# A linear-attention block with SwiGLU, forward and backward, on one core: warm-up and z inside the k/q loop, reloads moved to other queues, a ring filled ahead, a padded last K tile

## The chip, the cores and the metric

The kernel runs on one core of one Trainium2 chip. The metric is the device time of a whole execution in microseconds (us); lower is better. TensorE (PE) multiplies matrices and reads its left operand by separate weight loads (PEld), VectorE (DVE), ScalarE (ACT) and GpSimd (POOL) do elementwise work, and SyncE (SP), ACT and POOL issue DMAs from queues that run in order.

## The reference, cut to what matters

The input x has 2048 rows (S) of 640 features (D). There are 32 heads of 20 features, and F = 1728 hidden features.

```python
def A(x, wqkv, wo):                    # linear attention
    q, k, v = split_heads(x @ wqkv)
    pq, pk = phi(q), phi(k)            # phi(t) = where(t > 0, t + 1, exp(t)) + 1e-6
    kv = einsum("bhsd,bhse->bhde", pk, v)
    z = einsum("bhsd->bhd", pk)
    o = (pq @ kv) / (pq . z + 1e-6)    # per head and row
    return merge_heads(o) @ wo
def B(x, w_gate, w_up, w_down):
    return (silu(x @ w_gate) * (x @ w_up)) @ w_down
h = x + A(layernorm(x), wqkv, wo)
out = h + B(layernorm(h), w_gate, w_up, w_down)
```

The kernel returns `out` (out_0) and the gradients of x, wqkv, wo, w_gate, w_up and w_down for a given `grad_out`, all in bf16.

## The kernel before, in words

Rows are cut into 16 tiles of 128 (ST), features into 5 tiles (DT). A product with 640 output columns runs as two halves of 320 columns (`mm_row`, L115), each accumulated over its K tiles in one bank of a PSUM buffer; all matmuls share four such buffers. In SBUF, `strips` has four large buffers (tag S) and `big` five (tag B). The stages follow each other on TensorE:

- **k/q loop** (L256 to L268, 8.6 to 61.7 us). For each tile LayerNorm 1 (`ln_stats`, `ln_rstd`: VectorE's `lnv` L130, then POOL's power L131), the normalised `xn` (L226), five transposes `ps_t` (L230) copied by ScalarE, then k and q (`ps_kq`, 20 matmuls) and phi: two ScalarE operations per half of k/q from PSUM, two on VectorE. The order of PE, DVE and ACT is written out by hand. x's first tile is loaded first.
- **z and masks** (L270 to L278, 61.7 to 67.3 us). `ps_z` sums pk over all rows by 32 matmuls with a matrix of ones; five matmuls with E (the 0/1 matrix of heads, made on POOL, L185 to L190) make the head masks.
- **middle** (to 175 us). `ps_y`, `ps_kvt`, `ps_w2`, `ps_a` with LayerNorm 2, and between them `ps_dm`, the gradient of the product of gate and up; for groups 1 to 3 it is stored in `scr_dm`.
- **four F groups** (L403 to L487, 175 to 477 us) of 448, 448, 448 and 384 columns. A loop over pairs of tiles computes gate and up (`pg`, `pu`), four ScalarE operations and seven VectorE operations (L440 to L446) that make m, dg and du; dg and du (`dd`) are transposed on SP into `stg` (L449) and stored by POOL in `scr_dT` (L450). Then SP transposes the weights into `wgT` (L458), and `dw` (L460 to L473) multiplies, evicts `dwev` and stores it from POOL. A group after the first needs `dm_s`, loaded on SP at L410 in the group's first lines. `ps_dw` begins with m_s, so with 28 matmuls that don't need the loop's last pair.
- **dhn** (L534 to L579, 481 to 621 us). `cols`, the transposed dg and du of two tiles, is loaded on POOL (`load_cols`, L519); each tile is 54 matmuls with wgT, and lagging behind it `ps_dp`.
- **the small matrices** (to 656 us): `ps_gt`, `ps_dkvt`, `ps_wv2` (whose WV2 is transposed into WK2 on SP), then `ps_dz`, VectorE's `dzE` (L625) and `ps_dzb`.
- **dwqk, dk, dxn** (L630 to L698, to 798 us). `dwqk(0)` stores the gradient of wq; a loop over tiles makes dk (from `xnT_r`, loaded on ACT's queue, and `pkr`, loaded on POOL) and, three tiles later, `ps_dxn` from three transposed pieces in `ring` (dk four slots, pk and dq three each), all transposed by SP.
- **down** (L725 to L745, to 873 us): `ps_o` with 14 K tiles per half, the last of 64 rows (L734), `dwo` and `dwv` between the tiles.

Within the hand-ordered stretches the named engines keep the order of the code: PE, DVE and ACT in the k/q loop, PE and DVE in the middle, SP in the F groups and later. Otherwise a scheduler orders the instructions. DMAs of the hardware queues take turns over eight completion semaphores (lanes) in the order of the program, so a new one also waits for the earlier one on its lane.

Of the kernel before, what the change touches and what calls it, by code (L numbers as in the profile page):

```python
# [20 lines left out]
def kernel(  # L21
# [106 lines left out]
    def ln_rstd(mv, mean, rstd, t0, nt):  # L128
        v = small.tile([P, 4], FP32, name="lnv", tag="lnv")
        nc.vector.tensor_scalar(out=v[:, :nt], in0=mv[:, :nt, 1], scalar1=1e-5, scalar2=None, op0=ALU.add)  # L130
        nc.gpsimd.tensor_tensor(out=rstd[:, t0:t0 + nt], in0=v[:, :nt], in1=nhalf[:, :nt], op=ALU.pow)  # L131

    def ln_bwd(ps, xhat, rstd_col, resid, dst, pool):
# [10 lines left out]
        nc.vector.tensor_tensor(out=dst, in0=a[:], in1=resid, op=ALU.add)  # L144

# [28 lines left out]
    for t0 in range(4, ST, 2):  # L174
# [4 lines left out]
    ident = const.tile([P, P], BF16, name="ident")  # L179
    make_identity(nc, ident[:])  # L180
    nhalf = const.tile([P, 4], FP32, name="nhalf")
    nc.vector.memset(nhalf[:], -0.5)
    ones = const.tile([P, P], BF16, name="ones")
    nc.vector.memset(ones[:], 1.0)
    E = const.tile([H, D], BF16, name="E")  # L185
    nc.gpsimd.memset(E[:], 1.0)
    nc.gpsimd.affine_select(out=E[:], in_=E[:], pattern=[[1, D]], compare_op=ALU.is_ge,
                            fill=0.0, base=0, channel_multiplier=-Dh)
    nc.gpsimd.affine_select(out=E[:], in_=E[:], pattern=[[-1, D]], compare_op=ALU.is_ge,
                            fill=0.0, base=Dh - 1, channel_multiplier=Dh)  # L190
# [29 lines left out]
    def ln1_stats(t):  # L220
        mvs[t] = small.tile([P, 4, 2], FP32, name="mv", tag="mv")
        ln_stats(x_tm[t // 8][:, t % 8, :], mvs[t][:, 0, :])
        ln_rstd(mvs[t], None, rstd1, t, 1)
# [32 lines left out]
    with tc.manual_schedule(engines={EngineType.PE, EngineType.DVE, EngineType.Activation}):  # L256
        ln1_stats(0)
# [12 lines left out]
    ps = mm("ps_z")  # L270
    mm_row(ps, lambda t: ones[:], lambda t, n0, n1: pk[:, t, n0:n1], ST)
    nc.scalar.copy(out=half(zb[:]), in_=row(ps))

    for i in range(DT):
        e0, e1 = head_range(i)
        ps = mm("ps_mask")
        nc.tensor.matmul(ps[:, 0, :e1 - e0], lhsT=E[:, i * P:(i + 1) * P], rhs=E[:, e0:e1], start=True, stop=True)
        nc.scalar.copy(out=mask[:, i, :e1 - e0], in_=ps[:, 0, :e1 - e0])  # L278
# [55 lines left out]
    with tc.manual_schedule(engines={EngineType.PE, EngineType.DVE}):  # L334
# [35 lines left out]
        for t in range(ST + 2):  # L370
            if t < ST:
# [8 lines left out]
                ln_rstd(mv, None, rstd2, t, 1)  # L380
# [16 lines left out]
    with tc.manual_schedule(engines={EngineType.SP}):  # L397
# [5 lines left out]
        wgu = {0: load_wgu(0), 1: load_wgu(1)}  # L403
        for g in range(4):
            w = GW[g]
            if g == 0:
                dm_s = dm0
            else:
                dm_s = strips.tile([P, ST, GM], BF16, name="dm_s", tag="S")
                nc.sync.dma_start(out=dm_s[:, :, :w], in_=scr_dm_v[:, :, GO[g]:GO[g] + w])  # L410
# [5 lines left out]
            for t in range(0, ST, 2):  # L416
# [25 lines left out]
                nc.vector.tensor_tensor(out=du, in0=m, in1=dmv, op=ALU.mult)  # L442
                nc.vector.tensor_tensor(out=m, in0=m, in1=u, op=ALU.mult)  # L443
# [64 lines left out]
    with tc.manual_schedule(engines={EngineType.SP}):  # L508
# [6 lines left out]
        colp = {}  # L515
        pqr = {}
        dh1Ts = {}

        def load_cols(p):  # L519
            colp[p] = strips.tile([P, 2, NKT, P], BF16, name="cols", tag="S")  # L520
            nc.gpsimd.dma_start(out=colp[p][:], in_=scr_dT[2 * p:2 * p + 2].rearrange("t p k c -> p t k c"))
# [9 lines left out]
        load_cols(0)  # L531
# [80 lines left out]
        nc.gpsimd.dma_start(out=mat_v(scr_dKVT), in_=dKVT[:])  # L612
        wvk = strips.tile([P, 2, DT, D], BF16, name="wvk", tag="S")
# [8 lines left out]
        dzE = wk("dzE")  # L622
        ps = mm("ps_dz")
        mm_row(ps[:H], lambda t: nS1[:, t, :], lambda t, n0, n1: pqs_tm[:, t, n0:n1], ST)
        nc.vector.tensor_tensor(out=half(dzE[:H, :]), in0=row(ps)[:H], in1=half(E[:]), op=ALU.mult)  # L625
# [12 lines left out]

        G = mat("G")
        tr_mat(G, scr_GT)  # L640
# [4 lines left out]
        dwqk(0, 0, 4)  # L645

        dk = big.tile([P, ST, D], BF16, name="dk", tag="B")
        ring = strips.tile([P, 10, DT, P], BF16, name="ring", tag="S")
# [127 lines left out]
```

## Time and profile before

| | |
|---|---|
| median of 3 runs | 878.8 us (878.8 to 879.22) |
| the profiled execution, its own time | 884.85 us |
| its span in the profile | 883.0 us |
| mean granted TensorE clock | 0.980 |
| TensorE busy | 842.5 us, 95% |
| VectorE, ScalarE, POOL busy | 422.8, 299.8, 183.3 us |
| DMA traffic | 175.66 MB, 199 GB/s |

Times in the profile run from the start of the span. A row of a timeline gives start, length, engine, line, operation, output <- inputs and, in brackets, how long the engine sat idle ahead of it and what released it. A row of the waits gives the total, the number of times and the longest. A row of the chain gives start, length and what ran.

### The profile page before, as it was taken

How to read it: one execution, taken by the hardware profiler on the slowest of the kernel's cores; microseconds unless marked ns; L12 is line 12 of the kernel's file. 1: busy time of each engine (PE TensorE's matmuls, PEld its weight loads, DVE VectorE, ACT ScalarE, POOL GpSimd, SP SyncE). 2: the span in 40 equal slices, each digit the busy share in tenths (PEclk: the TensorE clock that was granted, in tenths of full speed). 3: DMA queues.
4: the chain of work that ended last, by engine and by line, in shares of the span. 5: the costliest groups of instructions: out<-in, count | busy, mean ns of one | idle time of the engine just before them, and what ended most of it. 6: DMA issues, size and time to landing. Idle time of an engine off the chain costs nothing.

```text
span 883.0 us, 13963 instructions
## 1 busy us (share of the span) xinstructions
PE 842.5 (95%) x5461; PEld 528.9 (60%) x5461; DVE 422.8 (48%) x864; ACT 299.8 (34%) x421; POOL 183.3 (21%) x321
## 2 busy tenths in 40 slices
PE   6999999999998899999998999999999699999995
PEld 4666655655554455555654777777766477776663
DVE  6969645886019405902910254786811366421111
ACT  5982433293157016513701222232221133331010
POOL 2110111213242331231225021111002111113140
PEclk9999999999999899999998999999999799999998
DMA  9999969999998893994799777773599699786971
GB/s 300 205 301 271 217 166 245 208 220 219 225 272 201 210 269 80 215 226 117 188 235 257 226 171 227 162 177 94 93 249 237 138 176 178 152 201 138 228 209 49
DMA packets 304066, 175.66 MB, mean 199 GB/s; under 512 B 250464, under 2 KB 289680, under 8 KB 304000
## 3 DMA queue, kind: packets, MB, share of 16 engines
q1 hardware_dynamic: 273856, 91.51, 52.8%
q0 software_dynamic: 19296, 72.60, 26.0%
q10 hardware_dynamic: 10848, 10.65, 4.3%
q8 instruction: 43, 0.70, 0.3%
q14 instruction: 23, 0.19, 0.1%
HBM read 53.72 MB, written 64.01 MB: 133 GB/s over the span
## 4 chain that ended last, share of the span: by engine, by line
PE 69%; DMA 14%; DVE 10%; issue 4%; ACT 1%; POOL 1%; SPq 0%; DVEq 0%; POOLq 0%; ACTq 0%
PE ps_dhn L119 14%; PE ps_dw L469 10%; PE ps_dxn L689 8%; PE ps_dm L293 7%; DMA stg<-dd 6%; PE ps_o L735 6%; PE ps_dwqk L119 4%; DMA scr_dT<-stg 3%; PE ps_gt L528 2%; PE ps_y L119 2%; PE ps_dp L119 2%; PE ps_a L119 2%; PE pg L420 2%; PE ps_dk L119 2%; PE pu L425 2%
## 5 line engine op out<-in xcount | busy, mean ns | idle before, releaser
L119 PE MATMUL ps_dhn<-wgT,cols 128*128 128x320 bf16 x864 | 122.0, 303 | 3.8 <-DMA cols<-scr_dT 3.8
L469 PE MATMUL ps_dw<-dd,hn 128*128 128x448 bf16 (+1 forms) x640 | 118.8, 346 | 0.0
L119 PEld LDWEIGHTS <-cols 128*128 128x128 bf16 x864 | 85.5, 99 | 38.4 <-DMA cols<-scr_dT 4.2
L469 PEld LDWEIGHTS <-hn 128*128 128x128 bf16 x640 | 62.6, 98 | 54.2
L471 ACT CAST dwev<-ps_dw 128x896 bf16<-128x896 f32 (+1 forms) x20 | 17.6, 878 | 164.7 <-PE ps_dw L469 155.1
L471 DVE CAST dwev<-ps_dw 128x896 bf16<-128x896 f32 (+3 forms) x12 | 10.9, 906 | 127.1 <-PE ps_dw L469 107.1
L469 PE MATMUL ps_dw<-m_s,dh 128*128 128x448 bf16 (+1 forms) x320 | 63.9, 357 | 7.2 <-DVE m_s L443 7.2
L735 PE MATMUL ps_o<-wd,mT 128*128 128x320 bf16 x448 | 67.7, 300 | 0.0
L450 POOL DMA_DIRECT2D scr_dT<-stg x64 | 34.6, 541 | 158.9 <-DMA stg<-dd 151.6
L689 PEld LDWEIGHTS <-ring 128*128 128x128 bf16 x480 | 48.1, 100 | 28.9 <-DMA ring<-dq 9.0
L420 PE MATMUL pg<-wgu,hnT 128*128 128x448 bf16 (+1 forms) x320 | 63.6, 346 | 0.0
L425 PE MATMUL pu<-wgu,hnT 128*128 128x448 bf16 (+1 forms) x320 | 63.6, 346 | 0.0
L293 PE MATMUL ps_dm<-wdT,dh2T 128*128 128x448 bf16 (+1 forms) x320 | 62.0, 346 | 0.0
L689 PE MATMUL ps_dxn<-wqkvT,ring 128*128 128x320 bf16 x320 | 53.3, 307 | 8.7 <-DMA ring<-dq 8.7
L735 PEld LDWEIGHTS <-mT 128*128 128x128 bf16 x448 | 41.3, 97 | 26.3 <-issue 8.4
L469 PEld LDWEIGHTS <-dh 128*128 128x128 bf16 x320 | 32.0, 100 | 37.1 <-issue 11.8
L425 PEld LDWEIGHTS <-hnT 128*128 128x128 bf16 x320 | 31.3, 98 | 27.1
L119 PE MATMUL ps_kq<-wqk,xnT 128*128 128x320 bf16 x320 | 47.5, 306 | 0.0
L420 PEld LDWEIGHTS <-hnT 128*128 128x128 bf16 x320 | 31.3, 98 | 27.1
L293 PEld LDWEIGHTS <-dh2T 128*128 128x128 bf16 x320 | 31.3, 98 | 25.1
L737 DVE TENSOR_TENSOR h1r<-ps_o,h1r 128x640 bf16<-128x640 f32 x16 | 13.2, 825 | 67.4 <-PE ps_o L735 62.6
L136 ACT ACTIVATE lb_dy<-ps_dhn,rstd 128x640 bf16<-128x640 f32 x16 | 12.7, 793 | 81.4 <-PE ps_dhn L119 81.4
(144 smaller groups left out, 1264.9 us busy)
## 6 DMA issues: line engine op xcount, KB each, us to landing
cols<-scr_dT POOLq DMA_DIRECT2D x8, 1728.0 KB, 9.2
scr_dT<-stg POOLq DMA_DIRECT2D x48, 224.0 KB, 2.8
scr_m<-m_s POOLq DMA_DIRECT2D x12, 448.0 KB, 4.3
scr_dm<-dmst ACTq DMA_DIRECT2D x16, 224.0 KB, 3.2
dm_s<-scr_dm SPq DMA_DIRECT2D x2, 1792.0 KB, 11.2
out_dram<-dwev POOLq DMA_DIRECT2D x30, 112.0 KB, 4.7
scr_dT<-stg POOLq DMA_DIRECT2D x16, 192.0 KB, 3.3
scr_xn<-xn SPq DMA_DIRECT2D x4, 640.0 KB, 5.7
```

What stands on the lines that cost most here:

```text
L119: nc.tensor.matmul(ps[:, ci, :320], lhsT=lhs(k), rhs=rhs(k, n0, n1), start=(start and k == 0), stop=(stop and k == n - 1))
L136: nc.scalar.activation(out=half(dy[:]), in_=row(ps), func=ACT.Copy, scale=rstd_col, accum_out=sums[:, 0:1])
L293: nc.tensor.matmul(ps[:, c, :w], lhsT=dh2T[:, kt, (t + c) * P:(t + c + 1) * P], rhs=wdT[g // 2][:, kt, o:o + w], start=(kt == 0), stop=(kt ...
L420: nc.tensor.matmul(pg[:, c, :w], lhsT=hnT[:, kt, (t + c) * P:(t + c + 1) * P], rhs=wg[:, kt, 0:w], start=(kt == 0), stop=(kt == DT - 1))
L425: nc.tensor.matmul(pu[:, c, :w], lhsT=hnT[:, kt, (t + c) * P:(t + c + 1) * P], rhs=wg[:, kt, w:2 * w], start=(kt == 0), stop=(kt == DT - 1))
L450: nc.gpsimd.dma_start(out=scr_dT[t + c, :, KO[g]:KO[g] + GK[g], :], in_=stg[:, :GK[g], :])
L469: nc.tensor.matmul(ps[:, c, :w], lhsT=lhs(t), rhs=rhs(t), start=(t == 0), stop=(t == ST - 1))
L471: copy(out=ev[:, :len(parts), :w], in_=ps[:, :len(parts), :w])
L528: nc.tensor.matmul(ps[:, ci, :320], lhsT=dh1[:, t, i * P:(i + 1) * P], rhs=pqs_tm[:, t, n0:n1], start=(t == 0), stop=(t == ST - 1))
L689: nc.tensor.matmul(ps[:, ci, :320], lhsT=lhs[:, i, :], rhs=rhs[:, i, n0:n1], start=(k == 0 and i == 0), stop=(k == 2 and i == DT - 1))
L735: nc.tensor.matmul(ps[:, ci, :320], lhsT=mT[:kk, t % 4, j, :], rhs=wd[:kk, j, n0:n1], start=(j == 0), stop=(j == FT - 1))
L737: nc.vector.tensor_tensor(out=half(h1r[:]), in0=row(ps), in1=half(h1r[:]), op=ALU.add)
```

## The change

In the k/q loop, 48 matmuls of the identity with itself (`ps_warm`, never read) run on TensorE before the first transposes. The mask matmuls move ahead of the first k/q matmul, all five into one PSUM buffer. `ps_z` is opened before the loop and two of its matmuls follow tile t's k/q matmuls from t = 2 on, so one of the four PSUM buffers is held throughout. POOL's order is written out for ident and E, and `lnv` goes from VectorE to POOL (but for the first two tiles).

In the F groups the load of `dm_s` for the next group, and after the last group the first `cols`, are issued on ACT's queue right behind the group's loop; `cols` of tile pair 1 stays on POOL. VectorE's seven operations are reordered with an extra work tile `a`, so that none directly follows one it depends on. It takes a third buffer of the six that nsg, u and `dwev` share.

`ps_dz` and dzE go ahead of `ps_wv2`. The pk and dq pieces of the ring for tiles 0 to 2 are issued before the loop, and those of tile u + 3 once tile u's matmuls are issued. G's transposes move into the loop, behind those of KV and Y. `dwqk(0)` is cut 3, 1, 1 instead of 4, 1. The last K tile of `ps_o` has 128 rows, of which 64 in `wd` are set to zero. The last tile of the output is added and stored in two halves, from ACT's and SP's queues.

```diff
+        eng.tensor_scalar(out=v[:, :nt], in0=mv[:, :nt, 1], scalar1=1e-5, scalar2=None, op0=ALU.add)
...
+        ps = mm("ps_warm")
+        for _ in range(48):
+            nc.tensor.matmul(ps[:, 0, :P], lhsT=ident[:], rhs=ident[:], start=True, stop=True)
...
+        ps_z = mm("ps_z")
+        def z_mm(t):
+            for ci, (n0, n1) in enumerate(NCH):
+                nc.tensor.matmul(ps_z[:, ci, :320], lhsT=ones[:], rhs=pk[:, t, n0:n1],
+                                 start=(t == 0), stop=(t == ST - 1))
...
+            if t == 0:
+                masks()
             kq_mm(t)
             if t > 0:
                 kq_phi(t - 1)
+            if t > 1:
+                z_mm(t - 2)
         kq_phi(ST - 1)
...
-                nc.sync.dma_start(out=dm_s[:, :, :w], in_=scr_dm_v[:, :, GO[g]:GO[g] + w])
...
+                a = fw("a")[:, :, :w]
                 nc.vector.tensor_tensor(out=m, in0=m, in1=dg, op=ALU.mult)
+                nc.vector.tensor_tensor(out=a, in0=u, in1=dmv, op=ALU.mult)
                 nc.vector.tensor_tensor(out=nsg, in0=nsg, in1=m, op=ALU.mult)
                 nc.vector.tensor_tensor(out=du, in0=m, in1=dmv, op=ALU.mult)
+                nc.vector.tensor_tensor(out=nsg, in0=nsg, in1=dg, op=ALU.add)
                 nc.vector.tensor_tensor(out=m, in0=m, in1=u, op=ALU.mult)
-                nc.vector.tensor_tensor(out=nsg, in0=nsg, in1=dg, op=ALU.add)
-                nc.vector.tensor_tensor(out=dg, in0=u, in1=dmv, op=ALU.mult)
-                nc.vector.tensor_tensor(out=dg, in0=dg, in1=nsg, op=ALU.mult)
+                nc.vector.tensor_tensor(out=dg, in0=a, in1=nsg, op=ALU.mult)
...
+            if g < 3:
+                dm_s = strips.tile([P, ST, GM], BF16, name="dm_s", tag="S")
+                act_load(dm_s[:, :, :GW[g + 1]], scr_dm_v[:, :, GO[g + 1]:GO[g + 1] + GW[g + 1]])
+            else:
+                load_cols(0, act_load)
...
+        for v in range(3):
+            load_pqT(v)
         G = mat("G")
-        tr_mat(G, scr_GT)
...
-                    kk = P if j < 13 else 64
-                    nc.tensor.matmul(ps[:, ci, :320], lhsT=mT[:kk, t % 4, j, :], rhs=wd[:kk, j, n0:n1],
+                    nc.tensor.matmul(ps[:, ci, :320], lhsT=mT[:, t % 4, j, :], rhs=wd[:, j, n0:n1],
```

How the queues stand, in three places. The first is the turn from group 0 to group 1. Before, SP's queue (`w2t` and `hnT` belong to the middle; x16 stands for a run of like instructions):

```order
L389 DMA_TRANSPOSE hnT<-hn 128x5x128 x3
L393 DMA_TRANSPOSE w2t<-W_1333 128x5x128 x3
L156 DMA wgu<-in_B_w_up_dram 128x5x448
L449 DMA_TRANSPOSE stg<-dd 128x7x128 x16
L458 DMA_TRANSPOSE wgT<-wgu 128x7x128 x5
L410 DMA dm_s<-scr_dm 128x16x448
L155 DMA wgu<-in_B_w_gate_dram 128x5x448
```

Now ScalarE's queue, at the end of group 0's loop (L464 to L467 are its four operations per pair, L508 the evictions of dw):

```order
L464 ACTIVATE dd<-pg 128x2x448
L465 ACTIVATE nsg<-pg 128x896
L466 CAST m_s<-pg 128x896
L467 CAST u<-pu 128x896
L149 DMA dm_s<-scr_dm 128x16x448
L508 CAST dwev<-ps_dw 128x896 x5
```

The load has left SP, where it stood behind the 16 stg and 5 wgT transposes, and stands on ACT ahead of the five evictions. The second place is SP's queue after dhn, before:

```order
L502 DMA_TRANSPOSE wqkvT<-in_A_wqkv_dram 128x5x128 x15
L621 DMA_TRANSPOSE wvk<-wvk 128x5x128 x5
L502 DMA_TRANSPOSE G<-scr_GT 128x5x128 x5
L670 DMA_TRANSPOSE ring<-dk 128x5x128 x2
L673 DMA_TRANSPOSE ring<-scr_pk 128x5x128
L674 DMA_TRANSPOSE ring<-dq 128x5x128
```

And SP's queue there now (L670 and L671 are the new `load_pqT`, L704 the dk pieces):

```order
L539 DMA_TRANSPOSE wqkvT<-in_A_wqkv_dram 128x5x128 x15
L653 DMA_TRANSPOSE wvk<-wvk 128x5x128 x5
L670 DMA_TRANSPOSE ring<-scr_pk 128x5x128
L671 DMA_TRANSPOSE ring<-dq 128x5x128
L670 DMA_TRANSPOSE ring<-scr_pk 128x5x128
L671 DMA_TRANSPOSE ring<-dq 128x5x128
L670 DMA_TRANSPOSE ring<-scr_pk 128x5x128
L671 DMA_TRANSPOSE ring<-dq 128x5x128
L704 DMA_TRANSPOSE ring<-dk 128x5x128 x4
```

Six pieces that stood behind dk's now stand ahead of them, where G's five were. The third place is POOL's queue at the same point, before:

```order
L602 DMA scr_GT<-GT 128x5x640
L612 DMA scr_dKVT<-dKVT 128x5x640
L637 DMA out_dram<-dwqk 128x640 x3
L653 DMA pkr<-scr_pk 128x640 x2
L637 DMA out_dram<-dwqk 128x640
```

And POOL's queue there now (L665 is the dwqk store, L687 the load of pkr):

```order
L630 DMA scr_GT<-GT 128x5x640
L640 DMA scr_dKVT<-dKVT 128x5x640
L687 DMA pkr<-scr_pk 128x640
L665 DMA out_dram<-dwqk 128x640 x2
L687 DMA pkr<-scr_pk 128x640 x2
L665 DMA out_dram<-dwqk 128x640
```

The first load of pkr has moved from behind three dwqk stores to ahead of all of them.

More of the change, by code (lines that the diff above doesn't have):

```diff
@@ L256, with masks @@
     with tc.manual_schedule(engines={EngineType.PE, EngineType.DVE, EngineType.Activation}):
+        def masks():
+            ps = mm("ps_mask")
+            for i in range(DT):
+                e0, e1 = head_range(i)
+                pm = ps[:, i // 3, (i % 3) * 160:(i % 3) * 160 + e1 - e0]
+                nc.tensor.matmul(pm, lhsT=E[:, i * P:(i + 1) * P], rhs=E[:, e0:e1], start=True, stop=True)
+            for i in range(DT):
+                e0, e1 = head_range(i)
+                pm = ps[:, i // 3, (i % 3) * 160:(i % 3) * 160 + e1 - e0]
+                nc.scalar.copy(out=mask[:, i, :e1 - e0], in_=pm)
+        ps = mm("ps_warm")
+        for _ in range(48):
+            nc.tensor.matmul(ps[:, 0, :P], lhsT=ident[:], rhs=ident[:], start=True, stop=True)
         ln1_stats(0)
@@ L267 @@
                 kq_phi(t - 1)
+            if t > 1:
+                z_mm(t - 2)
         kq_phi(ST - 1)
[L270 to L278, printed above, removed]
+        z_mm(ST - 2)
+        z_mm(ST - 1)
+        nc.scalar.copy(out=half(zb[:]), in_=row(ps_z))
     dm0 = strips.tile([P, ST, GM], BF16, name="dm0", tag="S")
@@ L612 @@
         nc.gpsimd.dma_start(out=mat_v(scr_dKVT), in_=dKVT[:])
+        dzE = wk("dzE")
+        ps = mm("ps_dz")
+        mm_row(ps[:H], lambda t: nS1[:, t, :], lambda t, n0, n1: pqs_tm[:, t, n0:n1], ST)
+        nc.vector.tensor_tensor(out=half(dzE[:H, :]), in0=row(ps)[:H], in1=half(E[:]), op=ALU.mult)
         wvk = strips.tile([P, 2, DT, D], BF16, name="wvk", tag="S")
```

89 lines of the change are left out of this document (44 added, 45 removed).

## The prediction

> **What bounds the kernel now.** I read the page first: the share of each engine, then the chain that ended last.
>
> ```profile
> span 883.0 us, 13963 instructions
> PE 842.5 (95%) x5461; PEld 528.9 (60%) x5461; DVE 422.8 (48%) x864; ACT 299.8 (34%) x421; POOL 183.3 (21%) x321
> ...
> PE 69%; DMA 14%; DVE 10%; issue 4%; ACT 1%; POOL 1%; SPq 0%; DVEq 0%; POOLq 0%; ACTq 0%
> ```
>
> TensorE is busy for 842.5 of 883.0 us, so only 40.5 us of idle time can be won, and beside it whatever makes busy time longer than it needs to be. Next I read TensorE's waits, which list whole stalls.
>
> ```profile
> PE ps_t L230 <- DVE xn L226: 9.0, 3, 6.9
> PE ps_dxn L689 <- DMA ring<-dq: 8.7, 1, 8.7
> PE ps_dw L469 <- DVE m_s L443: 7.2, 3, 3.5
> PE ps_dhn L119 <- DMA cols<-scr_dT: 3.8, 1, 3.8
> PE ps_dzb L119 <- DVE dzE L625: 0.9, 1, 0.9
> PE ps_mask L277 <- ACT zb L272: 0.5, 1, 0.5
> ```
>
> Columns: total us, times, longest. They make 30.1 us, and every row is one that the diff touches. A long stall costs twice: in two stretches of the windows view (length, then busy us and instructions of PE, PEld, DVE, ACT, POOL, then PEclk) the granted clock stands at half.
>
> ```profile
> 285.00:290.00 5.00, 0.91 (x2) 0.25 (x2) 4.93 (x10) 0.17 (x1) 1.08 (x2) 0.50 1.00 218
> ...
> 692.00:698.00 6.00, 5.97 (x23) 3.42 (x24) 0.00 (x0) 0.00 (x0) 0.00 (x0) 0.50 0.67 131
> ```
>
> **The start, z and the masks.** TensorE's timeline and the warm pace (a row of the chain):
>
> ```profile
> 6.86 0.72 PE L230 MATMUL ps_t<-ident,xn 128*128 128x128 bf16 x5 [6.86 <-DVE xn L226]
> ...
> 8.64 4.50 PE L119 MATMUL ps_kq<-wqk,xnT 128*128 128x320 bf16 x20
> ...
> 61.66 4.51 PE L119 MATMUL ps_z<-pk,ones 128*128 128x320 bf16 x32
> ...
> 67.31 2.88 PE L119 MATMUL ps_y<-pk,xn 128*128 128x320 bf16 x20
> ```
> ```profile
> 514.59 7.33 PE ps_dhn L119 x54
> ```
>
> A warm 320-column matmul takes 7.33/54 = 0.1357 us, so 20 take 2.71; the first 20 took 4.50, 1.8 more, at the cold clock. The k/q loop itself goes by VectorE:
>
> ```profile
> 33.07 0.88 DVE L125 BATCH_NORM_STATS2 st<-x_tm 128x6 f32<-128x320 bf16 x2
> ...
> 36.32 0.88 DVE L125 BATCH_NORM_STATS2 st<-x_tm 128x6 f32<-128x320 bf16 x2
> ```
> ```profile
> 36.40:39.65 3.25, 3.17 (x25) 2.15 (x25) 2.97 (x11) 3.18 (x5) 0.56 (x1) 1.00 1.01 197
> ```
>
> A tile takes 36.32 - 33.07 = 3.25 us. TensorE needs 2.71 plus five transposes (128/320 of 0.1357 each, 0.27), so 2.98; two z matmuls add 0.27 and make 3.25: z fits into the gap. ScalarE, 3.18 busy with its overlaps counted twice, is as near. Of the 5.65 us from 61.66 to 67.31 (z, masks, the 0.5 wait) six z matmuls (0.8) stay behind the loop: 4.85. The warm-up on ident fills the 6.86 us of waiting and gives up to 1.8. Against that, the masks now stand ahead of the first k/q matmul, and E is late on POOL:
>
> ```profile
> 7.18 0.71 POOL L189 TENSOR_SCALAR_AFFINE_SELECT E<-E 32x640 bf16<-32x640 bf16 x1
> ```
>
> Both of E's selects now follow the two rstd, so E is ready at 7.18 + 2 x 0.71 = 8.6, and five short mask matmuls put the first k/q matmul at about 9.3, 0.7 later than before. That is 4.85 + 1.1 = 6.0 at most, if the loop, near its VectorE limit, keeps all of the start; 3.5 if the three PSUM buffers that ps_z leaves cost 0.15 a tile. I take 5.3, nearer to the rows: ps_y at 62.0. Moving `lnv` from VectorE to POOL is in this term: POOL has 0.56 of 3.25 us busy and a tile of lead.
>
> **The F groups: dm_s.** The chain, VectorE's and TensorE's timelines around group 1:
>
> ```profile
> 253.16 10.97 DMA dm_s<-scr_dm
> ```
> ```profile
> 264.15 0.63 DVE L442 TENSOR_TENSOR dd<-m_s,dm_s 128x896 bf16<-128x896 bf16 x1 [7.71 <-DMA dm_s<-scr_dm]
> ```
> ```profile
> 286.07 0.91 PE L469 MATMUL ps_dw<-m_s,dh 128*128 128x448 bf16 x2 [3.46 <-DVE m_s L443]
> 290.06 6.48 PE L469 MATMUL ps_dw<-m_s,dh 128*128 128x448 bf16 x20 [3.09 <-DVE m_s L443]
> ```
>
> The load is issued on SP behind 16 stg and 5 wgT transposes, lands at 264.13, and VectorE, 7.71 late, makes TensorE wait 3.46 + 3.09. A 448-column matmul takes 448/320 of 0.1357, 0.19 us, warm, so two lost 0.53 and twenty 6.48 - 3.80 = 2.7 to the clock: 9.8 in all. The load now sits on ScalarE's queue right behind group 0's last u copy. There it waits for VectorE's last use of the loop and for the seventh stg transpose (its completion lane); queued behind it are the first dw evictions, which four PSUM buffers cover. So it leaves when less than half of the chain is done, lands long before group 1, and the stall goes. SP is free of it, and its stg and wgu of group 1 move up. What comes next is the traffic: 1792 KB now fall into the middle of the stg chain. The nearest rows are a 2560 KB load amid the same chain in group 3 (the DMA answer, us to landing last) and POOL's wait behind it:
>
> ```profile
> pqs_tm<-scr_pqs POOLq DMA_DIRECT2D x1, 2560.0 KB, 11.5
> ```
> ```profile
> 461.47 0.54 POOL L450 DMA_DIRECT2D scr_dT<-stg  x1 [10.79 <-DMA stg<-dd]
> ```
> ```profile
> 253.32 1.20 POOL L473 DMA_DIRECT2D out_dram<-dwev  x2
> ```
>
> That load stopped the chain for 10.79, of which about 8 is more than a usual step; by size 1792/2560 x 8 = 5.6. The dwev stores stand in POOL's queue behind the chain (last issue 253.32), and group 1's second pair needs their buffers back, since the new tile `a` makes three of six per pair. TensorE has about 3 us of cushion there, so 0 to 6.5 us of new stall; I take 3, near the middle. Net 6.8, from 3 to 9.8. In a sentence by itself: the Trainium skill, "Trainium Kernel Development and Optimization", Key Constraints, says that transfers from the SP, ACT and POOL queues share the same 16 DMA engines and interleave, so another issuing engine saves only issue time; by that alone this term would be near its lower end.
>
> Group 3 has the last of the ps_dw waits:
>
> ```profile
> 442.77 0.81 PE L469 MATMUL ps_dw<-m_s,dh 128*128 128x384 bf16 x4 [0.66 <-DVE m_s L443]
> ```
>
> Reordered, no VectorE operation follows directly on one that it depends on: 0.6, from 0 to 0.66.
>
> **cols.** The chain, TensorE and SP:
>
> ```profile
> 471.47 9.68 DMA cols<-scr_dT
> ```
> ```profile
> 481.19 10.99 PE L119 MATMUL ps_dhn<-wgT,cols 128*128 128x320 bf16 x61 [3.81 <-DMA cols<-scr_dT]
> ```
> ```profile
> 465.80 14.26 SPq L458 DMA_TRANSPOSE wgT<-wgu  x5
> ```
>
> The stall is 3.81 and the cold clock 10.99 - 61 x 0.1357 = 2.7: 6.5. cols(0) now goes out at about 444, right behind the m_s that ended the wait at 442.77, and lands before 481.19 - 3.81 = 477.4, where dw ends. Next late are group 3's wgT transposes, queued on SP behind the stg chain until 480.06: ps_dhn reads the last of them 48 matmuls (6.5 us) after its start, and the traffic ahead of them has grown by 1728 KB. I charge 3 us (0 to 9.5): net 3.5, from -3 to 6.5.
>
> **dz** ahead of wv2 hides the 0.9 us of dzE under wv2's matmuls (26 of them): 0.9 (0.5 to 1.2).
>
> **The ring.** The chain, and ScalarE:
>
> ```profile
> 676.80 7.90 DMA pkr<-scr_pk
> ...
> 688.14 3.85 DMA ring<-dq
> 692.03 7.16 PE ps_dxn L689 x30
> ...
> 700.55 4.07 PE ps_dxn L689 x30
> ```
> ```profile
> 669.81 1.88 ACT L636 CAST dwqk<-ps_dwqk 128x640 bf16<-128x640 f32 x3 [13.00 <-DMA G<-scr_GT]
> ```
>
> pkr is issued on POOL behind three dwqk stores, dk waits for it, and on SP the pk and dq transposes stand behind the dk transposes: TensorE waits 8.7 and then pays 7.16 - 4.07 = 3.1 of clock, 11.8. Now the pk and dq pieces of three tiles go ahead of dk, G's five transposes (read only by dwo, after the loop) go into the loop, and pkr(0) goes ahead of the stores. The new wait: ScalarE's xnT_r loads stand behind the wvk and the first ring transposes, the dwqk evictions behind those (13.00 already), so TensorE may wait about 1 us for PSUM. Taken 10.5 (8 to 11.8).
>
> **The padded last K tile.** Weight loads by form, and the chain:
>
> ```profile
> L735 PEld LDWEIGHTS <-mT 128*128 128x128 bf16 x416 | 38.3, 98 | 17.9
> ...
> L735 PEld LDWEIGHTS <-mT 64*128 64x128 bf16 x32 | 3.0, 92 | 8.4 <-issue 8.4
> ```
> ```profile
> 806.11 46.34 PE ps_o L735 x308
> ```
>
> Each 64-row load sat 8.4/32 = 0.26 us idle ahead of itself, and the pace is 46.34/308 = 0.1505 instead of 0.1357: 0.0148 x 448 = 6.6 us, gone if all loads have 128 rows. The memset of 64 rows lies in VectorE's idle time. So 6.6 (0 to 6.6).
>
> **The tail.** The last tile's add follows TensorE alone:
>
> ```profile
> 873.50 0.82 DVE L737 TENSOR_TENSOR h1r<-ps_o,h1r 128x640 bf16<-128x640 f32 x1 [3.40 <-PE ps_o L735]
> ```
>
> In halves, the first lies under the second half's matmuls: 0.4, and a little from two queues: 0.5 (0 to 1.5).
>
> **Sum.** 5.3 + 6.8 + 0.6 + 3.5 + 0.9 + 10.5 + 6.6 + 0.5 = 34.7 us. The profiled execution took 884.85 (span 883.0 and 1.85 around it), 6.05 over the median of 878.8; it would take 850.2, and the median 844.1.
>
> **Rivals.** (1) The DMA queue takes the place of the waits: dm_s's early load and cols(0) only push stg, dwev and wgT back. For it: the 10.79 row. Against it: the same bytes move in the end, and TensorE has work there. dm_s falls to 1.5 and cols to 0: 8.8 less, 852.9; chance 0.25. (2) The padding brings nothing, because the 0.26 us comes from the accumulation's end and not from the row count: 844.1 + 6.6 = 850.7. Against it: the loads of 128 rows show 17.9/416 = 0.04 us of idle each, and ps_dhn, whose 54 matmuls end two accumulations too, runs at 0.1357 all the same. Chance 0.08. Beside it: the Trainium skill, "TensorE: Matmul & The Clock Gate", LDWEIGHTS, says that a load of fewer rows takes as long as one of 128; the loads agree (92 and 98 ns), and a rule by row count alone would give this rival's time, but the idle time ahead is beside that rule. (3) The ring's fill is early but dk is not: if xnT_r comes 8 us late, dk(0) is what ps_dxn waits for, and 8 of the 10.5 stay: 852.1; for it speaks the 13.00 row, against it that the loads start earlier than dk needs them. Chance 0.10. (4) Slower: in the k/q loop ps_z holds one of four PSUM buffers, and a buffer of ps_kq is written in 1.36 (10 matmuls) and read by two ScalarE operations of about 0.64 (3.18/5), 2.6 of a period of 3.25. Should that chain reach past the period by more than 34.7/16 = 2.2 us a tile, the kernel is slower; matmul and reads wholly in turn cost 2 x 1.28 = 2.6 a tile, 41 us: 885. There is some 0.6 us of slack, so chance 0.02. The forecast keeps 0.55.
>
> **Numbers.** The likeliest is the sum, 844.1. All terms at their good ends make 44.1 us, 834.7, which needs all of them at once: the range begins at 836. Rivals 1 to 3 reach 853, two of them together 859 to 861. So 836 to 859, which leaves out about 0.15. Terms in the bad half of their bounds without a rival (3 in the loop, 1.5 at the ring, 2 for cols) lie inside it. A measurement of this kernel tells 0.2% (1.8 us) from no change. Faster 0.97, same 0.01, slower 0.02 (rival 4 and several losses at once).
>
> **What would show it.** In the changed profile: ps_y at 62 and no ps_z group behind the loop; no TensorE wait for m_s in group 1 (if one for wgu, dwev or PSUM stands there, rival 1); ps_dhn's wait for cols gone, or changed to wgT; ps_dxn starting within 2 us of the last dk; the pace of ps_o at 0.136 and no 64-row loads. I am wrong if the k/q loop's period is over 3.4, or if a half-clock stretch still stands at 285, 481 or 692 less the shift.

## The result and the profile after

The changed kernel takes 0.9661 of the time before, with a 95% interval from 0.9577 to 0.9745: 844.42 to 853.59 us, the middle one 849.51, where the kernel before takes 878.8 to 879.22. The forecast was 844.1, a ratio of 0.9605, inside the interval. Executions that ran disturbed (here one of 872.78 us) are left out of such ratios, and of the six profiles taken in an execution over 860 us (pad_undone, ring_late, no_warm, g_back, tail_pool, bridge_wgt) only the stretches named below are used. The profiled execution took 849.51, its span is 847.8. The page's first lines:

```profile
span 847.8 us, 14044 instructions
PE 831.8 (98%) x5509; PEld 534.3 (63%) x5509; DVE 415.6 (49%) x836; ACT 299.4 (35%) x421; POOL 191.8 (23%) x349
```

The span is 35.2 us shorter: 24.5 of TensorE's 40.5 us of idle time are gone, and 10.7 of its busy time although 48 matmuls came in. What it still waits for:

```profile
PE ps_dhn L119 <- DMA wgT<-wgu: 3.0, 1, 3.0
PE ps_t L243 <- DVE xn L239: 1.5, 2, 0.8
PE ps_warm L284 <- POOL ident masks.py:199: 1.4, 1, 1.4
PE ps_dw L506 <- DVE m_s L475: 1.3, 3, 0.7
PE ps_dwv L750 <- DVE h1r L768: 1.2, 1, 1.2
PE ps_o L765 <- DMA mT<-scr_m: 0.8, 1, 0.8
PE ps_dwqk L119 <- DVE tk L702: 0.7, 1, 0.7
```

The waits for the ring, for cols and for dzE are no longer there, and five of the seven are new: wgT, h1r, mT, tk, and ident, for which the warm-up itself waits. TensorE's timeline at the places of the forecast:

```profile
9.25 4.21 PE L119 MATMUL ps_kq<-wqk,xnT 128*128 128x320 bf16 x20
...
62.63 7.63 PE L119 MATMUL ps_y<-pk,xn 128*128 128x320 bf16 x55
...
278.49 3.19 PE L506 MATMUL ps_dw<-m_s,dh 128*128 128x448 bf16 x16 [0.33 <-DVE m_s L475]
282.36 0.92 PE L506 MATMUL ps_dw<-m_s,dh 128*128 128x448 bf16 x4 [0.69 <-DVE m_s L475]
...
463.54 3.02 PE L119 MATMUL ps_dhn<-wgT,cols 128*128 128x320 bf16 x21
...
469.54 10.71 PE L119 MATMUL ps_dhn<-wgT,cols 128*128 128x320 bf16 x66 [2.98 <-DMA wgT<-wgu]
...
667.73 0.84 PE L717 MATMUL ps_dxn<-wqkvT,ring 128*128 128x320 bf16 x5
```

In group 1 the waits are short and the matmuls behind them warm. ps_dhn now stands, after 21 matmuls, for wgT in the place of cols, and 66 matmuls that need 9.1 us take 10.7 behind it (66 x 0.1357, and 0.17 for the last one to end, as 20 warm ones take 2.88 us and not 2.71). ps_dxn starts without a wait.

This table cuts the span where TensorE changes its work; each figure is a difference of two starts in its timeline (the last line: from TensorE's end to the span's). It shows where the 35.2 us came from. There is one profile of each kernel here, and the one before is of an execution 6 us over the median.

| stretch | before | after | gain | forecast |
|---|---|---|---|---|
| start to ps_y | 67.31 | 62.63 | 4.7 | 5.3 |
| ps_y to group 1's loop | 182.84 | 182.83 | 0.0 | 0 |
| group 1's loop to group 2's | 85.58 | 77.00 | 8.6 | 6.8 |
| group 2's loop to group 3's dw | 101.66 | 101.67 | 0.0 | 0 |
| group 3's dw to the first ps_dp | 75.68 | 73.48 | 2.2 | 0.6 + 3.5 |
| ps_dp to ps_dzb | 142.57 | 141.70 | 0.9 | 0.9 |
| ps_dzb to the first ps_o | 142.55 | 131.65 | 10.9 | 10.5 |
| ps_o to TensorE's end | 75.22 | 71.01 | 4.2 | 6.6 |
| TensorE's end to the span's | 9.59 | 5.83 | 3.8 | 0.5 |

### The profile page after: what moved, and what is told of

Same layout as the page of the kernel before. It is cut to its first block, busy times and chain, and to the rows that moved or that the text cites. A ratio compares the mean times of both kernels' runs of the same rounds, so it can differ in the third digit from the quotient of the medians.

```text
span 847.8 us, 14044 instructions
## 1 busy us (share of the span) xinstructions
PE 831.8 (98%) x5509; PEld 534.3 (63%) x5509; DVE 415.6 (49%) x836; ACT 299.4 (35%) x421; POOL 191.8 (23%) x349
## 5 line engine op out<-in xcount | busy, mean ns | idle before, releaser
L508 DVE CAST dwev<-ps_dw 128x896 bf16<-128x896 f32 (+3 forms) x12 | 10.9, 909 | 134.7 <-PE ps_dw L506 82.1
L508 ACT CAST dwev<-ps_dw 128x896 bf16<-128x896 f32 (+1 forms) x20 | 17.6, 878 | 163.7 <-PE ps_dw L506 129.2
L765 PE MATMUL ps_o<-wd,mT 128*128 128x320 bf16 x448 | 61.5, 299 | 0.8 <-DMA mT<-scr_m 0.8
L506 PE MATMUL ps_dw<-m_s,dh 128*128 128x448 bf16 (+1 forms) x320 | 60.8, 346 | 1.3 <-DVE m_s L475 1.3
L765 PEld LDWEIGHTS <-mT 128*128 128x128 bf16 x448 | 43.8, 98 | 18.1 <-DMA mT<-scr_m 1.2
L717 PE MATMUL ps_dxn<-wqkvT,ring 128*128 128x320 bf16 x320 | 51.3, 299 | 0.0
## 6 DMA issues: line engine op xcount, KB each, us to landing
dm_s<-scr_dm ACTq DMA_DIRECT2D x2, 1792.0 KB, 10.5
```

The costliest lines, as they stand in the source:

```text
L506: nc.tensor.matmul(ps[:, c, :w], lhsT=lhs(t), rhs=rhs(t), start=(t == 0), stop=(t == ST - 1))
L508: copy(out=ev[:, :len(parts), :w], in_=ps[:, :len(parts), :w])
L717: nc.tensor.matmul(ps[:, ci, :320], lhsT=lhs[:, i, :], rhs=rhs[:, i, n0:n1], start=(k == 0 and i == 0), stop=(k == 2 and i == DT - 1))
L765: nc.tensor.matmul(ps[:, ci, :320], lhsT=mT[:, t % 4, j, :], rhs=wd[:, j, n0:n1], start=(j == 0), stop=(j == FT - 1))
```

## The experiments

Each is the changed kernel with one edit. All are read by these stretches, since whole executions of one kernel lie 9 us apart (the changed kernel) and more (11 us in dve_before). A stretch that an edit leaves alone varies too: in the profiles below, group 1 with the new order and the early load takes 75.67 to 82.59 us; ps_dzb to the first ps_o takes 130.78 to 132.78 where the edit lies elsewhere, but 135.08 in pad_undone and 144.48 in bridge_wgt.

**pad_undone**

```diff
-                    nc.tensor.matmul(ps[:, ci, :320], lhsT=mT[:, t % 4, j, :], rhs=wd[:, j, n0:n1],
+                    kk = P if j < 13 else 64
+                    nc.tensor.matmul(ps[:, ci, :320], lhsT=mT[:kk, t % 4, j, :], rhs=wd[:kk, j, n0:n1],
```

> The changed kernel, but the last K tile of ps_o has 64 rows again. Theory: the 64-row weight loads cost 0.0148 us per matmul, 6.6 us over the 448, but in the changed kernel part of what they gave back was lost again to the h1r loads and mT (waits of 1.2 and 0.8 us in its profile), so undoing it costs 3.5 to 5 us from the first ps_o to the last, with 32 loads at 0.26 us of idle each and no wait for h1r left. Rival (row count of a weight load does not matter): ps_o takes as long as in the changed kernel, 71 us from first to last, within 1 us.

The weight loads by form (busy, mean ns, idle before) in this kernel and then in the changed one:

```profile
L766 PEld LDWEIGHTS <-mT 128*128 128x128 bf16 x416 | 38.3, 98 | 17.9
...
L766 PEld LDWEIGHTS <-mT 64*128 64x128 bf16 x32 | 3.0, 93 | 8.4 <-issue 8.4
```
```profile
L765 PEld LDWEIGHTS <-mT 128*128 128x128 bf16 x448 | 43.8, 98 | 18.1 <-DMA mT<-scr_m 1.2
```

From the first ps_o to TensorE's end it took 75.22 us, to the hundredth what it took before the change, against 71.01 with the padding. 32 loads more of 128 rows add 0.2 us of idle time, not 8.4. The theory holds, and the rival falls with the prediction's second one. Kernels with the padding took 68.6 to 72.1 there, but for two (74.4 in g_back, 76.0 in h1r_pools): where nothing is late, as in dve_before with 68.62, the whole 6.6 us of the forecast is there.

**loads_back**

```diff
-            if g < 3:
-                dm_s = strips.tile([P, ST, GM], BF16, name="dm_s", tag="S")
-                act_load(dm_s[:, :, :GW[g + 1]], scr_dm_v[:, :, GO[g + 1]:GO[g + 1] + GW[g + 1]])
-            else:
-                load_cols(0, act_load)
...
+            if g > 0:
+                dm_s = strips.tile([P, ST, GM], BF16, name="dm_s", tag="S")
+                nc.sync.dma_start(out=dm_s[:, :, :w], in_=scr_dm_v[:, :, GO[g]:GO[g] + w])
...
+        load_cols(0)
         load_cols(1)
```

> The changed kernel, but dm_s is loaded on SP in the group's first lines and the first cols on POOL, as before the change. Theory: the place of the dm_s load alone makes the gain in group 1, so the waits of ps_dw for m_s come back to 6 to 7 us with a half-clock stretch, and group 2 begins 8 to 9 us later than in the changed kernel; the first ps_dhn waits for cols or for wgT and begins 1 to 3 us later still: 9 to 12 us in all. Rival (the traffic is the limit and the early load is paid for elsewhere; VectorE's new order makes up for the rest): at most 4 us.

Its ratio to the kernel before is 0.9743 (0.9692 to 0.9795); its four executions took 855.13 to 863.15 us, a median of 859.0. TensorE's waits and timeline there:

```profile
PE ps_dhn L119 <- DMA cols<-scr_dT: 6.4, 1, 6.4
PE ps_dw L504 <- DVE m_s L478: 4.3, 3, 3.3
```
```profile
282.61 3.19 PE L504 MATMUL ps_dw<-m_s,dh 128*128 128x448 bf16 x16 [3.33 <-DVE m_s L478]
286.48 0.92 PE L504 MATMUL ps_dw<-m_s,dh 128*128 128x448 bf16 x4 [0.68 <-DVE m_s L478]
...
474.23 11.03 PE L119 MATMUL ps_dhn<-wgT,cols 128*128 128x320 bf16 x63 [6.41 <-DMA cols<-scr_dT]
```

Group 1 took 81.88 us (77.00 in the changed kernel, 85.58 before), group 3's dw to the first ps_dp 77.63 (73.48; 75.68). So the two loads' places are worth 4.9 + 4.2 = 9.0 us, at the low end of the theory's 9 to 12, but in other parts: the theory had 8 to 9 in group 1 and 1 to 3 at ps_dhn. Its fastest execution (855.13) is slower than the slowest counted one of the changed kernel (853.59). In group 1 the wait comes back, 4.0 of the 4.3 us above where the theory had 6 to 7, and no half-clock stretch with it (16 matmuls in 3.19 us are warm); the missing half-clock stretch, 3.2 us by the prediction's count, is most of the 3.7 us to the kernel before. VectorE waits 6.48 for dm_s there, against 7.71; that its new order then catches up sooner is argued, not shown.

**ring_late**

```diff
-        for v in range(3):
-            load_pqT(v)
...
                 nc.sync.dma_start_transpose(out=ring[:, t % 4], in_=dk[:, t, :])
+            if 0 <= t - LAG + 2 < ST:
+                load_pqT(t - LAG + 2)
...
-            if u + 3 < ST:
-                load_pqT(u + 3)
```

> The changed kernel, but the pk and dq pieces of the ring are issued where they were before the change, behind each tile's dk piece; pkr's early load, G's place in the loop and the dwqk cut 3, 1, 1 stay. Theory A (the fill ahead makes the gain): ps_dxn waits 4 to 9 us for ring<-dq again, with the clock at half behind it. Theory B (the early pkr and the dwqk pieces between the first dk do it): dk and its pieces are early anyway, the pk and dq pieces land before the second dwqk piece ends, and ps_dxn starts within 1 us of the changed kernel.

```profile
PE ps_dxn L717 <- DMA ring<-dq: 0.9, 1, 0.9
```

That is the only wait for the ring. The ratio to before is 0.9699 (0.9642 to 0.9757), and from ps_dzb to the first ps_o it took 131.82 us (131.65 in the changed kernel); ps_dxn starts 27.55 us after ps_dzb, and 28.42 in the changed kernel. Theory B holds: the fill ahead, by which the prediction explained this gain, brings nothing here. The next two take the rest apart.

**dwqk_41** and **g_back** both keep that edit. The first:

```diff
-        dwqk(0, 0, 3)
+        dwqk(0, 0, 4)
...
-            if t in (2, 3):
-                dwqk(0, t + 1, t + 2)
+            if t == 2:
+                dwqk(0, 4)
```

> The changed kernel with the ring's pk and dq pieces behind dk's as before, and with dwqk(0) cut 4, 1 as before, by which pkr's first load stands behind three dwqk stores on POOL again; G's transposes stay inside the loop. Theory C (G's transposes held up ScalarE's xnT_r loads, and with them the evictions, the stores and pkr): G's place alone makes the gain, ps_dzb to the first ps_o takes 131 to 133 us as in the changed kernel (131.7). Theory D (the cut and the early pkr make it): the wait for the ring comes back, 4 to 9 us, and with the clock the stretch takes 137 to 142 us (142.6 before the change).

The second:

```diff
         G = mat("G")
+        tr_mat(G, scr_GT)
...
-            if 3 <= t < 3 + 3 * DT:
-                tr_piece((KV, Y, G)[(t - 3) // DT], (scr_KVT, scr_Yt, scr_GT)[(t - 3) // DT], (t - 3) % DT)
+            if 3 <= t < 3 + 2 * DT:
+                tr_piece((KV, Y)[(t - 3) // DT], (scr_KVT, scr_Yt)[(t - 3) // DT], (t - 3) % DT)
```

> The changed kernel with the ring's pk and dq pieces behind dk's and G's five transposes ahead of the loop, both as before; dwqk(0) stays cut 3, 1, 1 and pkr's first load early. Theory C (G's place makes the gain): the wait for the ring or for the dwqk evictions comes back, 4 us or more, and ps_dzb to the first ps_o takes 136 us or more. Theory D (the cut and the early pkr make it): it takes 131 to 134 us.

TensorE's timeline at the first ps_dxn, of dwqk_41 and then of g_back:

```profile
673.87 0.85 PE L717 MATMUL ps_dxn<-wqkvT,ring 128*128 128x320 bf16 x5 [1.74 <-DMA ring<-dq]
```
```profile
675.47 0.85 PE L718 MATMUL ps_dxn<-wqkvT,ring 128*128 128x320 bf16 x5 [2.61 <-DMA ring<-dq]
676.16 1.38 PE L718 MATMUL ps_dxn<-wvk,ring 128*128 128x320 bf16 x5
677.34 2.70 PE L718 MATMUL ps_dxn<-wqkvT,ring 128*128 128x320 bf16 x10
```

With G out of the way alone the stretch takes 133.08 us, with the cut and the early pkr alone 135.88 (g_back's 2.6 us wait is followed by matmuls at half pace). Against the 142.55 before, G's place alone brings 9.5 of the 10.9 us and the cut with pkr alone 6.7; they overlap. Both theories miss their ranges by a little (133.08 where C had 131 to 133, 135.88 where C had 136 or more and D 131 to 134), and each is one profile; that G's place is the larger part is likely, and not certain. How G did it is seen on ScalarE: before the change its first dwqk evictions stood to 669.81 behind xnT_r loads that waited 13.00 for G's transposes. In dwqk_41 the first one runs freely behind its matmuls:

```profile
649.35 0.69 ACT L664 CAST dwqk<-ps_dwqk 128x640 bf16<-128x640 f32 x1 [3.49 <-PE ps_dwqk L119]
```

In the changed kernel the ring's early pieces stand in G's old place and hold ScalarE again, and the 0.7 us of the dwqk wait, which ring_late does not have, may be its price:

```profile
651.76 1.91 ACT L664 CAST dwqk<-ps_dwqk 128x640 bf16<-128x640 f32 x3 [11.00 <-DMA ring<-scr_pk]
```

**no_warm**

```diff
-        ps = mm("ps_warm")
-        for _ in range(48):
-            nc.tensor.matmul(ps[:, 0, :P], lhsT=ident[:], rhs=ident[:], start=True, stop=True)
```

> The changed kernel without the 48 warm-up matmuls on the identity. In the changed kernel the first 20 k/q matmuls took 4.21 us at a granted clock of 0.50, against 4.50 before, so theory: the warm-up brings 0.3 us or nothing, and ps_y starts within 0.5 us of 62.6. Rival (the warm-up makes the start faster as forecast): the transposes and masks take 0.5 us longer and ps_y starts 1 to 2 us later.

**warm_bridge**

```diff
-        for _ in range(48):
-            nc.tensor.matmul(ps[:, 0, :P], lhsT=ident[:], rhs=ident[:], start=True, stop=True)
...
+        warm(54)
         ln1_stats(0)
         ln1_stats(1)
         ln1(0)
+        warm(12)
...
             if t == 0:
+                warm(5)
                 masks()
```

> The changed kernel with more warm-up matmuls: 54 instead of 48 at first, 12 between the first and the second transposes and 5 ahead of the masks. The first 20 k/q matmuls took 4.21 us in the changed kernel and 2.89 in two variants with the same start. Theory (the 3 us of little work between the warm-up and the first k/q matmul let the clock fall, in some runs): they take 2.9 us and ps_y starts at 60.5 to 61.5. Rival (the clock at the start goes by something else than TensorE's own work): they take 4.2 us or more and ps_y starts at 62.5 or later.

The first 20 k/q matmuls, of no_warm and then of warm_bridge, there with the filler ahead of them:

```profile
9.01 4.65 PE L119 MATMUL ps_kq<-wqk,xnT 128*128 128x320 bf16 x20
```
```profile
6.87 0.83 PE L287 MATMUL ps_warm<-ident 128*128 128x128 bf16 x12
...
8.14 0.44 PE L287 MATMUL ps_warm<-ident 128*128 128x128 bf16 x5
...
8.93 2.89 PE L119 MATMUL ps_kq<-wqk,xnT 128*128 128x320 bf16 x20
```

no_warm's ratio is 0.9616 (0.9565 to 0.9668), the changed kernel's within the interval. ps_y starts at 62.82 without the warm-up, at 62.63 with it in the changed kernel's profile, and at 60.98 with the bridge: both theories hold for these profiles. But the start with the 48 matmuls and no bridge is not always cold: in eight more profiles with the same 48 matmuls (pad_undone, loads_back, ring_late, dwqk_41, g_back, wgt_ahead, dve_before, h1r_pools) ps_y came at 60.9 to 61.9, and in tail_pool at 62.94. Against those eight the warm-up brings 0.9 to 1.9 us, as no_warm's rival had it. The bridge was seen twice, here and in bridge_wgt, at 60.98 and 61.3; with eight warm starts of ten without it, that it keeps the clock is not shown. The windows of the changed kernel (PEclk is the third column from the end) show a start that fails:

```profile
4.00:6.50 2.50, 2.04 (x26) 1.86 (x23) 2.36 (x9) 0.00 (x0) 0.71 (x2) 1.00 1.06 388
6.50:9.20 2.70, 1.56 (x15) 1.06 (x15) 1.95 (x5) 1.38 (x2) 2.09 (x4) 0.88 1.07 362
9.20:11.20 2.00, 2.00 (x9) 1.14 (x9) 1.24 (x3) 1.01 (x5) 0.61 (x2) 0.50 1.08 365
```

The transposes at 6.68 and 7.95 us took 0.45 us a set, as in the loop (0.71 to 0.72 without the warm-up), so the warm-up had brought the full pace; it was lost in the stretch with 1.56 busy of 2.70 us, just ahead of the work it was meant for. The busy share does not decide it: in dve_before the clock lasts with 1.53.

```profile
6.50:9.20 2.70, 1.53 (x17) 1.04 (x18) 1.98 (x5) 1.42 (x3) 2.09 (x4) 1.00 1.06 365
```

What decides it was not found. PEclk is not to be read alone this early: it stands at 1.00 from 9.20 to 11.20 in no_warm too, where 9 matmuls take the 2.00 us as they do here.

**wgt_ahead**

```diff
             m_s = strips.tile([P, ST, GM], BF16, name="m_s", tag="S")
...
+            if g == 3:
+                tr_wg()
...
-            k0, r0 = divmod(KO[g], 14)
-            for kt in range(DT):
-                nc.sync.dma_start_transpose(out=wgT[k0][:, r0:r0 + GK[g], kt * P:(kt + 1) * P], in_=wg[:, kt, 0:2 * w])
+            if g < 3:
+                tr_wg()
```

> The changed kernel, but group 3's five wgT transposes are issued on SP ahead of its stg transposes instead of behind them. In the changed kernel SP did nothing from 389 to 405 us, and the first ps_dhn waited 2.98 us for wgT there and 10.8 to 15.8 us in three runs of its variants. Theory (the wait for wgT at the end of the SP queue is what is left of the cols term, and what makes the runs differ): the wait for wgT goes, the time from the start of group 3's dw to the first ps_dp falls from 73.5 to 68.5 to 70 us, and all runs lie within 5 us of each other near 845. Rival (the DMA engines are full there, so something else of the same stage is late, cols or the stores): the wait only changes its name and the stage stays over 72 us.

The wait for wgT is gone, and group 3's dw to the first ps_dp takes 68.77 us, 4.7 less than the 73.48 of the changed kernel; with the 2.2 gained there that is 6.9 of the 7.1 (6.5 and group 3's 0.6) that the prediction saw in this stretch. But the time is 846.73 to 854.55, ratio 0.9652 (0.9591 to 0.9714): not to be told from the changed kernel by intervals as wide as the gain, and not within the 5 us that the theory said. In the profile group 1, which lies ahead of what was edited, took 80.82 us instead of 77.00, so this is scatter of group 1 and no price of the edit:

```profile
PE ps_dw L513 <- DVE m_s L483: 2.9, 4, 1.6
PE pg L456 <- DVE dwev L515: 1.6, 1, 1.6
```

**dve_before** tests the price in group 1.

```diff
-                a = fw("a")[:, :, :w]
...
-                nc.vector.tensor_tensor(out=a, in0=u, in1=dmv, op=ALU.mult)
...
+                nc.vector.tensor_tensor(out=dg, in0=u, in1=dmv, op=ALU.mult)
+                nc.vector.tensor_tensor(out=dg, in0=dg, in1=nsg, op=ALU.mult)
```

> The changed kernel with VectorE's seven operations of the F groups in the order of before and without the tile `a`, so that a pair takes two of the six shared buffers instead of three. Between the first loop matmul of group 1 and that of group 2 the changed kernel took 77.0 us in its profile and 75.7 to 81.1 in seven variants, where waits for dwev, m_s and for ScalarE appear; 75.7 is what TensorE alone needs. Theory (the third buffer per pair makes group 1's second pair wait for the dwev stores behind the stg chain, as charged): no wait for dwev in group 1, and 76 to 78 us in spite of the slower order; the wait ahead of group 3's last m_s returns to 0.6. Rival (the traffic of dm_s alone sets what is left, whatever the buffers): waits for dwev or ScalarE stay, 78 to 82 us.

```profile
PE ps_dw L504 <- DVE m_s L471: 3.0, 4, 1.1
PE pg L448 <- DVE dwev L506: 2.6, 1, 2.6
```

Group 1 took 82.32 us, with a longer wait for dwev although a pair takes two buffers again. So the wait does not need the third buffer, which the prediction named; that the stores behind the stg chain are late fits, but was not tried by itself, and VectorE's slower order is undone together with the buffer. The whole takes 847.97 to 859.15, ratio 0.9679 (0.9583 to 0.9776), which does not tell it from the changed kernel.

**tail_pool**

```diff
-                    (nc.scalar, nc.sync)[ci].dma_start(out=o0_v[:, t, n0:n1], in_=h1r[:, n0:n1])
+                    nc.gpsimd.dma_start(out=o0_v[:, t, n0:n1], in_=h1r[:, n0:n1])
```

> The changed kernel, but both halves of the last output tile are stored from POOL instead of ACT's and SP's queues. From TensorE's last matmul to the end of the span it took 9.6 us before the change and 5.8 now, 3.8 less, of which the halved add explains 0.4. Theory (the queue makes the rest: a store from POOL takes longer to issue and to be over): 9 us or more. Rival (the half-sized transfers make it): 6 to 7 us.

The last instructions, of this kernel and then of the changed one:

```profile
861.24 0.89 DVE L772 TENSOR_TENSOR h1r<-ps_o,h1r 128x320 bf16<-128x320 f32 x2 [2.98 <-PE ps_o L765]
862.03 1.07 POOL L773 DMA_DIRECT2D out_dram<-h1r  x2 [2.93 <-DVE h1r L772]
```
```profile
842.06 0.89 DVE L772 TENSOR_TENSOR h1r<-ps_o,h1r 128x320 bf16<-128x320 f32 x2 [2.98 <-PE ps_o L765]
842.58 0.36 ACTq L773 DMA_DIRECT2D out_dram<-h1r  x1
842.98 0.37 SPq L773 DMA_DIRECT2D out_dram<-h1r  x1
```

TensorE's end to the span's end is 10.05 us with POOL and 5.83 with ACT and SP; from the last issue to the span's end it is 871.2 - 863.10 = 8.1 against 847.8 - 843.35 = 4.5. Before the change, with one store of the whole tile from POOL, it was 883.0 - 875.16 = 7.8. The queue makes it, as the theory said.

**h1r_pools**

```diff
-            h1r = wk("h1r")
+            h1r = wk("h1r", pool=t % 2)
```

> The changed kernel, but the h1r tiles of ps_o take turns between two pools (5 and 7 buffers), so that their loads no longer wait for the store of an earlier output tile. From the first ps_o to TensorE's end the changed kernel took 71.0 us, of which waits are 0.8 (mT) and 1.2 (h1r); seven variants with the padding took 69.0 to 74.4 there, and the padding alone would make 75.2 - 6.6 = 68.6. Theory (the loads of h1r behind the stores on POOL take back part of the padding's gain): no wait for h1r and 68.6 to 69.8 us. Rival (the DMA engines are late with mT and h1r alike): 70.5 us or more.

```profile
PE ps_o L765 <- DMA mT<-scr_m: 5.2, 2, 4.2
```

No wait for h1r is left, but mT is 5.2 us late and the stretch took 75.98. The theory falls and the rival's number holds; its reason, that the DMA engines are late with mT and h1r alike, is argued from this one profile.

**bridge_wgt** joins warm_bridge and wgt_ahead.

> The changed kernel with both edits that helped a stage: the longer warm-up (ps_y at 61.0) and group 3's wgT transposes ahead of its stg (68.8 us from group 3's dw to the first ps_dp). Theory (what is left of the traffic's price sits in group 1 and in the waits for hnT and mT, and goes by how the DMA engines fall in each execution): the span is 841 to 848, by group 1 taking 75.7 to 81, and timed executions scatter between 843 and 852, 2 to 4 us under the changed kernel's and without its executions over 860. Rival (removing the wait for wgT makes no difference to the whole, since what is behind it is late in turn): the same 844 to 854 as the changed kernel, with single executions over 860.

Ratio 0.9617 (0.9571 to 0.9663), from five executions of 842.95 to 853.04 us with a middle of 848.34, so not distinguishable from the changed kernel; two more took 860.21 and 863.37. In the profile, which is of the last, ps_y came at 61.3 and the cols stretch took 68.77 as expected, and as in wgt_ahead, but another place was late:

```profile
PE ps_dwqk L119 <- DVE tk L716: 7.3, 1, 7.3
PE pg L463 <- DVE dwev L522: 2.9, 1, 2.9
PE ps_o L779 <- DMA mT<-scr_m: 2.9, 2, 2.0
```

The rival is nearer. The wait for tk lies in ps_dzb to the first ps_o, 144.48 us here and so longer than before the change. The chain that held the ring before is seen there again, with the ring's early pieces in G's place (SP's, ScalarE's and VectorE's timelines):

```profile
637.08 16.19 SPq L667 DMA_TRANSPOSE wvk<-wvk  x5
...
657.66 1.88 ACT L678 CAST dwqk<-ps_dwqk 128x640 bf16<-128x640 f32 x3 [16.96 <-DMA ring<-scr_pk]
...
671.80 0.77 DVE L712 TENSOR_SCALAR pkr<-pkr 128x640 bf16<-128x640 bf16 x2 [22.43 <-DMA pkr<-scr_pk]
```

The five wvk transposes, which take 7.74 us on SP in the changed kernel, take 16.19, and all behind them is late. What sends the DMAs late in one execution and not in the next was not found.

## Why the prediction was right, point by point

- **The sum** came to 34.7 and the profiles differ by 35.2 us, but in part by luck: of the seven rows of the table with a forecast five are within 2 us, and the misses of the other two, 2.4 and 3.3, have opposite signs. Between the medians lie only 878.8 - 849.51 = 29.3 us. The step that failed is the subtraction of 6.05 us to get from the profiled execution to the median. It held the changed kernel's runs to be as far below its profile; in fact the profiled 849.51 is the middle of them, so the median came out 5.4 us above 844.1. Which of the waits were larger than usual in the profile before is open, since there is one such profile. The 0.2% that a measurement was to tell was too fine as well: the ratio's interval reaches 0.84% to either side.
- **Start, z, masks** (5.3; measured 4.7): the z matmuls fit into the loop as computed, ps_y at 62.63 instead of 62.0, and with the clock held 60.9 (6.4, a little over the upper bound of 6.0). What was taken for a fixed 1.8 us is a matter of whether the clock lasts from the warm-up to the first k/q matmul; and it is 1.6, since 4.50 must be set against the 2.88 that 20 warm matmuls take, not against 2.71.
- **dm_s** (9.8 less 3): 8.6 in the profile, where the charge was 1.3. Over the five profiles below 860 us with the early load and the new order (77.0, wgt_ahead 80.8, warm_bridge 75.7, dwqk_41 78.8, h1r_pools 77.0) the stretch is 77.8 on average, 2.2 above the 75.67 of group 2: the charge had about the right size. Its reason was half wrong: the waits for dwev are there in some profiles, but they come without the third buffer too. And 3.7 of the gain do not need the load's new place, by the one profile of loads_back.
- **cols** (3.5, with group 3's 0.6; measured 2.2 for both): what the prediction named as next late, wgT behind the stg chain on SP, is what ps_dhn waits for, 2.98 us and then 1.6 us of clock; in the four other profiles below 860 us with the same order on SP (dwqk_41, warm_bridge, dve_before, h1r_pools) the stretch took 70.8 to 73.0, a gain of 2.7 to 4.9. It waits 21 matmuls after the start, at the first K tile that group 3 fills, and not 48.
- **dz** (0.9): 0.87.
- **The ring** (10.5): 10.9, for another reason. The step that failed is that pk and dq pieces behind dk's made the wait. What released it was the chain G, xnT_r, dwqk eviction, dwqk store, pkr, and either moving G or cutting dwqk with an early pkr breaks most of it, as far as one profile of each shows.
- **The padding** (6.6): mechanism and size right, and the Trainium skill's rule on row counts ("TensorE: Matmul & The Clock Gate", LDWEIGHTS) holds here for the load alone (93 and 98 ns), not for the idle time ahead of it (0.26 us for each of the 64-row loads). 4.2 were left after waits for mT and h1r, which the prediction did not have.
- **The tail** (0.5): 3.8. The term was mis-sized, since only the add was counted; the queue of the store is 3.6 of it.
- **The rivals.** The first (the DMA queue takes the place of the waits) came in part: wgT, dwev, mT and h1r are new waits, one or another of them in nearly every profile. In the changed kernel's profile, though, its two terms kept 10.8 us with group 3's, as in the sum (10.9), where this rival left 2.1. The second fell with pad_undone. The third (an early ring and a late dk) is not what the changed kernel's profile shows, but it is what bridge_wgt's shows, where the whole gain of that stretch is gone. The fourth did not come: no wait for PSUM is seen in the k/q loop, and its tiles follow each other by 3.27 us (the sum had 3.25):

```profile
52.39 0.44 PE L243 MATMUL ps_t<-ident,xn 128*128 128x128 bf16 x5
...
55.66 0.44 PE L243 MATMUL ps_t<-ident,xn 128*128 128x128 bf16 x5
```

## What to carry to other kernels

A late DMA is worth tracing back through every in-order queue that it crosses before choosing what to move: here the visible late transfer (the ring's pieces) was innocent, and transposes whose result is read only much later (G) held ScalarE, then POOL's queue, then VectorE. Where single executions of one kernel lie 9 us apart, an edit worth 5 us in its stretch is lost in the whole time, so judge it by its own stretch and by several profiles, and look whether a loss lies ahead of the edit or behind it. A warm-up brings its gain only in the executions in which the clock lasts to the first real matmul.

## What the runs showed of the hardware

- The clock gained by 48 matmuls at 1.4 to 6 us was lost again ahead of the first k/q matmul in two of ten profiles of the same instructions (0.50 from 9.2 us on in the changed kernel's), with 58% of the stretch ahead busy, and it lasted with 57% in dve_before. With more matmuls in the gaps it lasted in both profiles that had them, which does not show that they were needed.
- From the last issue of a store to the end of the span, POOL's queue took 8.1 us where ACT's and SP's took 4.5, for the same 128x320 tiles (one profile of each).
- A weight load of 64 rows takes about as long as one of 128 (93 and 98 ns), but the load queue sits idle for 0.26 us ahead of each, 6.3 to 6.6 us in a stretch with next to no other waits (75.22 us with them, 68.95 to 68.62 without).
